# A gated attention and GLU kernel: key weights on one DMA queue, another order of the first key products, a shorter warm-up

## The chip, the cores and the metric

The kernel runs on one core of a Trainium2 chip. The metric is the device time of one execution in microseconds. The kernel before was run three times: 264.33, 264.85 and 264.85 us, median 264.85 us. The profile is of a further execution of 264.76 us, whose span (from the first to the last instruction that the profile shows) is 263.0 us, so 1.76 us of it lie around the span.

## The reference

`x` has 2048 tokens of 512 features, bfloat16. The output is a mixture per token of an attention with a memory (`a`) and a gated feed-forward layer (`b`):

```python
g = sigmoid((x * gate_w).sum(-1, keepdims=True))
out = g * a + (1 - g) * b
# a: 32 heads of 16, four segments of 512 tokens
q, k, v = x @ wq, x @ wk, x @ wv              # split into heads and segments
for s in range(4):
    a_dot = softmax(qs @ ks.T * scale + causal_mask) @ vs      # inside the segment
    a_mem = phi(qs) @ M / (phi(qs) @ z + 1e-6)                 # from earlier segments
    o = sigmoid(beta) * a_mem + (1 - sigmoid(beta)) * a_dot
    M, z = M + phi(ks).T @ vs, z + phi(ks).sum()
a = o @ wo
# b: 1792 hidden features
b = (gelu(x @ w_gate) * (x @ w_up)) @ w_down
```

## The kernel before

All the work is cut into named tasks, each a few instructions of one engine, and a string `ORDER` at the end of the file (L861) lists every task once. Each engine gets its tasks in that order and works them off strictly one after another; semaphores between the engines are derived from what each instruction reads and writes. A suffix in the string gives a choice: `xev0_0:d` puts the task on VectorE (`a` would be ScalarE), `K0_1a:1` takes PSUM bank 1. So the order is written out by hand, and nothing moves by itself. All loads start in SyncE's queue (SP) but two, which ScalarE's queue (ACT) starts.

The four segments go through the same stages: K, Q and V projections (`K`, `Q`, `V`), scores and exponentials (`st`, `exp`), products with V (`pv`), gate and up projections of the feed-forward part (`G`, `U`), down projection and output (`wo`, `out`, `oev`, `dma`). The string interleaves them, so that TensorE has dense products between the small ones of the attention.

The change lies in the head, the first 16 us, which only segment 0 has:

- The first half of the tokens of segment 0 is loaded straight, 128 tokens by SP (`ld_x0_0`) and 128 by ACT (`ld_x0_1`), L356 to L357. TensorE turns it: `xtr0_1`, the feature blocks 2 and 3, then `xtr0_0`, the blocks 0 and 1 (L785). The copies `xev0_1` and `xev0_0` carry the turned blocks from PSUM to `xT` (L793 on ScalarE, L794 on VectorE).
- The second half of these tokens comes by two transposing DMAs of SP, `ld_x0_t2` and `ld_x0_t3` (L361).
- The key weights `wk` come in two halves (L358): `ld_wk1` holds the feature blocks 2 and 3, `ld_wk0` the blocks 0 and 1.
- Behind them SP starts `ld_wq0`, `ld_wq1` (query weights, L364), `ld_gw` (`gate_w`, L363, which must wait until VectorE has zeroed `omem`, the task `gwz`, L354), `ld_beta` (L367, waits until wk0 has landed), `ld_wv` (L366, waits until `x0_t3` has landed), `ld_wg0` (the first half of the gate weights, 896 KB, L369, waits until wq1 has landed) and four transposing loads of the next segment's tokens (`ld_x1_*`, L345, wait until wq0 has landed).
- While nothing has landed TensorE multiplies constants, `warm1` before the turning and `warm2` behind it (L380 to L382).
- The keys of segment 0 (`K0_t`, L471 to L476) are made for four feature groups t in three parts each: `a` takes the blocks 2 and 3 (and so wk1 and `xev0_1`) for the first 256 tokens, `b` the blocks 0 and 1 (wk0 and `xev0_0`), `c` all four blocks for the other 256 tokens. That is 8 + 8 + 16 matmuls of 256 columns. `evict` (L441, L442) takes the sums out of PSUM.

Behind the keys TensorE does `Q0_0`, `Q0_1` (L448), the first scores `st0_0A` (L601), `gwtr`, `Q0_3`, then V products (L498), `st0_0B`, more V products, and then `G0_6` (L448), the first product that reads `wg`. TensorE's order does not let anything behind `G0_6` start ahead of it.

```python
    for eng, h in ((SP, 1), (ACT, 0)):
        ld_w(f"wk{h}", eng, wk[:, halves[h], :], wsrc(A_wk)[:, halves[h], :], [("wk", 2 * h), ("wk", 2 * h + 1)], 0.25)
```

Of the kernel before, what the change touches and what calls it, by code (L numbers as in the profile page):

```python
# [248 lines left out]
def _build(es, nc, A_x, A_wq, A_wk, A_wv, A_wo, A_beta, B_w_gate, B_w_up, B_w_down, gate_w, out):  # L249
# [30 lines left out]
    ident = sb("ident", [P, P])  # L280
# [77 lines left out]
    for eng, h in ((SP, 1), (ACT, 0)):  # L358
        ld_w(f"wk{h}", eng, wk[:, halves[h], :], wsrc(A_wk)[:, halves[h], :], [("wk", 2 * h), ("wk", 2 * h + 1)], 0.25)
# [21 lines left out]
    for name, n, cols in (("warm1", 45, 80), ("warm2", 7, 80)):  # L381
        one(name, PE, 3.0, [I(lambda e, cols=cols: e.matmul(BK[s0.i][:, 0:cols], ones, ones[:, 0:cols], start=True, stop=True),  # L382
                              [], [bk(s0)]) for _ in range(n)], bias=9000.0, opens=name == "warm1")
# [478 lines left out]
ld_x0_0 ld_wk1 ld_x0_1 warm1:0 ident xtr0_1 xev0_1:d xtr0_0 warm2 xev0_0:d vones0 masks ld_wk0 causal1 gwz ld_x0_t2  # L862
ld_x0_t3 ld_wq0 ld_wq1 ld_gw ld_beta causal0 consts K0_1a:1 K0_3a:2 K0_3b K0_2a:3 K0_0a:0 K0_2b K0_0b K0_1b K0_0c
K0_2c K0_3c K0_1c Kev0_0:d Kev0_2:d kpadb0_0 kpadb0_2 causal kpada0_0 Kev0_3:a Q0_0:0 Qev0_0:a Q0_1:3 st0_0A gwtr:2
Kev0_1:d gwev Q0_3:0 ld_wv ld_wg0 Qev0_1:d V0_1b:1 V0_3a:2 V0_3b:3 exp0_0A Qev0_3:d Vev0_3a:a Vev0_1b:a st0_0B
Vev0_3b:d kpada0_2 kpada0_1 V0_0b:0 V0_1a:2 V0_2a:1 Vev0_0b:d G0_6:3 Gev0_6:d Vev0_1a:d Vev0_2a:d exp0_0B st0_0C
exp0_0C Q0_2:0 G0_2:3 V0_2b:2 ld_x1_2 ld_x1_1 betab ld_x1_3 ld_x1_0 st0_0D Vev0_2b:a exp0_0D Gev0_2:d kpadb0_1
Qev0_2:d phka0_0 V1_2b:1 V0_0a:3 G1_6:2 V1_0b:0 Vev1_2b:d phka0_2 st0_0E Vev0_0a:d Vev1_0b:d G0_1:1 bexp Gev1_6:a
exp0_0E Gev0_1:d Q1_2:3 V1_3b:2 V1_3a:0 kpada0_3 Qev1_2:d Vev1_3a:d phkb0_2 phkc0_2 Vev1_3b:d st0_1A gz0 gqa exp0_1A
gr0 Q1_0:1 V1_0a:3 G1_5:0 Vev1_0a:d gqb Gev1_5:d st0_1B Q1_1:2 K1_0:3 exp0_1B phkb0_0 ld_wu1 ld_x2_0 G0_5:0 Qev1_0:d  # L870
kpadb0_3 vsh0_21 st0_1C exp0_1C Qev1_1:d ld_x2_1 ld_x2_3 ktr0_3 ld_wg1 Gev0_5:d V1_2a:1 K1_3:2 K1_1:0 vsh0_01
Vev1_2a:a vsh0_20 ld_x2_2 ktr0_2 vsh0_00 ld_wd1 st0_1D phkc0_0 Kev1_1:d kpada1_1 G0_4:1 G0_3:0 Gev0_4:d Kev1_0:d
Gev0_3:d Kev1_3:a ld_wd0 ld_wu0 ktr0_1 ktr0_0 vsh1_20 ld_wo V1_1a:2 Vev1_1a:d exp0_1D st0_2A exp0_2A msk0_0B msk0_0D
msk0_0C kpada1_0 msk0_0E goa0 gob0 msk0_0A msk0_1A msk0_1C msk0_1D gfull msk0_1B G0_0:1 Q1_3:3 G1_1:0 Qev1_3:d phqa1_0
st0_2B Gev0_0:d Gev1_1:a pv0_1:2301 exp0_2B tp0_d01 tp0_d00 pvp0_01 Q2_0:3 Qev2_0:d tp0_d11 st0_2C K1_2:2 Kev1_2:d
pvp0_00 tp0_d10 gelu0 G0_8:3 G0_13:1 gd0_13 G0_10:2 G0_11:0 G0_9:1 gd0_8 gd0_10 gd0_9 gd0_11 G0_12:3 G0_7:2 gd0_12
G1_2:1 U0_0:0 gd0_7 Gev1_2:d pvp0_11 h0_0 U0_13:3 U0_10:2 h0_10 Q2_1:1 Qev2_1:d exp0_2C st0_2D mz0:0 U0_7:2 U0_9:1
pvp0_10 h0_13 exp0_2D phqb1_0 st0_2E exp0_2E phka1_0 h0_7 mza0 h0_9 ota0_0 phqa1_2 kpadb1_0 G1_4:3 U0_1:2 h0_1
Gev1_4:a V1_1b:0 st0_3A G1_0:1 U0_5:3 Q2_2:2 exp0_3A Vev1_1b:a Gev1_0:a Qev2_2:a kpadb1_1 st0_3B exp0_3B U0_11:0
U0_4:1 U0_12:2 st0_3C phkb1_0 exp0_3C phqc1_0 kpada1_2 h0_4 h0_5 U0_6:1 U0_2:3 h0_11 h0_12 phqb1_2 h0_2 G1_3:0  # L880
Gev1_3:d h0_6 kpadb1_2 st0_3D phka1_2 U0_3:2 h0_3 U0_8:3 h0_8 Q2_3:0 Qev2_3:d exp0_3D phkb1_2 msk0_2A msk0_2B msk0_2C
msk0_3A msk0_2E msk0_2D msk0_3C goc0 msk0_3B st1_0A msk0_3D pv0_3:1230 exp1_0A st1_0B exp1_0B tp0_d20 tp0_d21 pvp0_20
tp0_d30 ota0_1 pvp0_21 tp0_d31 kpada1_3 out0_1_0:1 out0_1_1 out0_1_2 V2_0a:2 Vev2_0a:d G1_9:3 V2_1b:0 Vev2_1b:d
wev0_1:d st1_0C G1_8:2 G1_10:0 G1_11:1 gelu1 gd1_9 G1_7:3 gd1_8 gd1_10 gd1_7 gd1_11 G1_13:2 gd1_13 G1_12:0 gd1_12
phqc1_2 phkc1_0 mzq0 pvp0_31 pvp0_30 ota0_3 V2_0b:3 Vev2_0b:d ota0_2 V2_1a:1 Vev2_1a:d out0_0_0:2 out0_0_1 out0_0_2
nd1_0:0 ndp1_0 phkc1_2 exp1_0C st1_0D exp1_0D K2_0:3 K2_2:1 wev0_0:d Kev2_0:d Kev2_2:a K2_1:0 st1_0E Kev2_1:d U1_2:2
h1_2 wo0_1:1 nd1_3:3 nd1_1:0 exp1_0E st1_1A ld_x3_2 vsh1_00 vsh2_01 ktr1_1 ktr1_0 oev0_1 ndp1_1 wo0_0:2 oev0_0
kpada2_0 vsh1_21 out0_2_0:1 nd1_2:0 msk1_0C msk1_0A exp1_1A st1_1B exp1_1B msk1_0B gz1 msk1_0E msk1_1A msk1_0D msk1_1B
out0_2_1 wo0_2:2 ndp1_2 st1_1C exp1_1C nd1_5:0 out0_2_2 ndp1_3 wev0_2:a ndp1_5 out0_3_0:3 st1_1D nd1_4:0 out0_3_1
out0_3_2 ktr1_2 dma0 vsh1_01 otr1_3 ndp1_4 otr1_0 oev0_2 phka2_0 msk1_1C wev0_3:d ktr1_3 dma1 vsh2_00 otr1_1 ld_x3_1  # L890
ld_x3_0 ld_x3_3 exp1_1D st1_2A exp1_2A gr1 msk1_1D pv1_1:1023 st1_2B exp1_2B tp1_d01 tp1_d00 kpadb1_3 V2_2b:0
Vev2_2b:d K2_3:1 Kev2_3:a G2_3:0 pvp1_00 Gev2_3:d tp1_d10 st1_2C U1_8:1 G2_1:0 otr1_2 V2_3a:2 h1_8 Gev2_1:d Vev2_3a:d
kpadb2_0 kpadb2_1 exp1_2C st1_2D phkb2_0 exp1_2D G2_6:1 wo0_3:0 U1_3:2 pvp1_01 tp1_d11 Gev2_6:a h1_3 phka2_2 oev0_3
st1_2E U1_0:3 V2_3b:1 G2_0:2 Gev2_0:d h1_0 Vev2_3b:d exp1_2E phkb2_2 st1_3A mz1:0 G2_4:2 G2_5:3 pvp1_10 mza1 Gev2_5:d
exp1_3A st1_3B exp1_3B Gev2_4:d U1_11:1 G2_2:0 Gev2_2:d ota1_0 U1_13:3 h1_13 U1_10:2 h1_10 h1_11 G2_11:0 G2_10:3
pvp1_11 phkc2_0 phkc2_2 ota1_1 otm1_0 otm1_1 G2_12:2 G2_9:1 st1_3C gelu2 gd2_11 gd2_12 G2_7:0 G2_13:2 gd2_10 gd2_9
gd2_7 gd2_13 G2_8:3 gd2_8 U1_7:1 U2_9:0 K3_0:2 h1_7 U2_5:3 Q3_0:1 phqa2_0 h2_9 h2_5 Qev3_0:d Kev3_0:d exp1_3C st1_3D
exp1_3D U1_1:0 U2_12:3 msk1_3A msk1_2A msk1_3B U2_13:1 h2_12 h1_1 h2_13 kpada2_1 st2_0A U1_9:2 V2_2a:3 U2_7:0 msk1_2D
msk1_2B msk1_2E h1_9 Vev2_2a:d vsh2_20 dma2 dma3 ktr2_0 ktr2_2 vsh2_21 exp2_0A phqb2_0 msk1_3D msk1_2C msk1_3C st2_0B
h2_7 kpada2_2 pv1_3:1230 tp1_d21 exp2_0B tp1_d20 V3_1a:2 Vev3_1a:a st2_0C exp2_0C pvp1_21 tp1_d31 U1_6:1 Q3_1:2  # L900
V3_0a:0 st2_0D h1_6 pvp1_20 Vev3_0a:d Qev3_1:a V3_2b:1 U1_4:2 U1_5:0 exp2_0D st2_0E exp2_0E tp1_d30 phqc2_0 h1_5 h1_4
ota1_2 Vev3_2b:a U1_12:3 h1_12 pvp1_31 pvp1_30 out1_1_0:0 st2_1A V3_1b:2 out1_1_1 V3_3a:3 exp2_1A st2_1B msk2_0B
msk2_0D Vev3_3a:a exp2_1B out1_1_2 U2_4:1 msk2_0E goa1 gob1 kpadb2_3 kpada2_3 msk2_0C msk2_0A msk2_1A ota1_3 h2_4
otm1_2 otm1_3 K3_1:3 mzq1 Vev3_1b:a wev1_1:a st2_1C msk2_1B goc1 U2_1:2 Q3_3:1 V3_0b:0 Kev3_1:d kpada3_0 h2_1 Qev3_3:d
kpadb2_2 exp2_1C msk2_1C st2_1D V3_2a:3 U2_6:2 exp2_1D Vev3_2a:a wo1_1:1 Vev3_0b:d kpadb3_0 h2_6 oev1_1 st2_2A msk2_1D
pv2_1:0231 exp2_2A st2_2B exp2_2B tp2_d00 pvp2_00 phqa2_2 tp2_d01 tp2_d10 pvp2_10 pvp2_01 tp2_d11 out1_0_0:0 out1_0_1
st2_2C phqb2_2 out1_0_2 V3_3b:2 Vev3_3b:d wev1_0:d out1_3_0:3 phqc2_2 pvp2_11 exp2_2C st2_2D exp2_2D wo1_0:1 out1_3_1
st2_2E nd2_0:2 out1_2_0:0 out1_3_2 msk2_2C gz2 gr2 gz3 gr3 goa3 ndp2_0 gob3 oev1_0 msk2_2D goc3 goa2 gob2 exp2_2E
st2_3A exp2_3A msk2_3A msk2_2B wev1_3:d G3_4:2 nd2_2:1 out1_2_1 Gev3_4:a ndp2_2 st2_3B exp2_3B nd2_4:3 G3_1:1 Gev3_1:d
out1_2_2 nd2_1:2 st2_3C dma4 ktr2_1 vsh3_20 vsh3_01 ktr2_3 dma5 ndp2_4 ndp2_1 G3_3:1 wo1_3:3 exp2_3C Gev3_3:a K3_2:2  # L910
st2_3D wev1_2:a msk2_2A kpada3_1 oev1_3 Kev3_2:d nd2_5:1 nd2_3:3 G3_0:0 G3_5:2 ndp2_3 ndp2_5 Gev3_0:d msk2_3C msk2_2E
exp2_3D st3_0A exp3_0A goc2 msk2_3D msk2_3B G3_2:3 wo1_2:1 Gev3_2:d G3_6:0 Gev3_6:a Gev3_5:d oev1_2 ota2_0 st3_0B
pv2_3:3210 exp3_0B tp2_d20 tp2_d21 K3_3:3 Kev3_3:a pvp2_20 pvp2_21 U2_3:2 tp2_d30 h2_3 st3_0C U2_8:3 U2_0:1 tp2_d31
otr2_2 otr2_0 dma6 dma7 otr2_1 vsh3_00 otr2_3 vsh3_21 h2_0 ota2_1 G3_7:2 G3_12:0 G3_10:1 gelu3 gd3_7 h2_8 ota2_2
# [11 lines left out]
ndp3_4 ota3_1 dma11 otr3_2 otr3_1 otr3_3 otr3_0 pv3_3:1203 tp3_d20 tp3_d21 pvp3_20 pvp3_21 tp3_d30 tp3_d31 ota3_2  # L926
pvp3_31 pvp3_30 otm3_1 otm3_0 ota3_3 out3_0_0:1 out3_2_0:2 out3_0_1 out3_2_1 out3_3_0:0 out3_0_2 out3_3_1 wev3_0:a
otm3_2 otm3_3 wo3_0:3 dma10 oev3_0 dma12 wo3_1:1 out3_2_2 out3_3_2 wo3_2:3 oev3_1 wev3_2:a oev3_2 wo3_3b:1 dma13 dma14
wev3_3:a oev3_3b dma15b wo3_3a:2 oev3_3a dma15a
"""  # L930


# [26 lines left out]
```

## Time and profile before

| what | value |
|---|---|
| median of three runs (range) | 264.85 us (264.33 to 264.85) |
| profiled execution | 264.76 us |
| its span | 263.0 us |
| TensorE matmul busy | 255.4 us, 97% of the span |
| ScalarE, VectorE, GpSimd busy | 203.1, 197.7, 98.7 us |
| chain that ended last: TensorE, DMA, ScalarE, VectorE | 86%, 4%, 3%, 3% of the span |
| HBM read, written | 7.87 MB, 2.10 MB |
| first K0 matmul, first `G0_6` matmul | 5.20 us, 15.86 us from the start of the span |

Times on the page and in the views are in microseconds from the start of the span. A line of the timeline has the start, how long it lasted, the engine (SPq and ACTq are the queues that start DMAs), the line of the kernel, the operation, what it writes and reads, and in brackets the idle time of the engine ahead of it and what ended it. The chain of waits goes back from the last instruction to whatever released each step. A matmul's duration covers its way through the array, and matmuls overlap, so the distance from start to start tells their rate.

### The profile page before, as it was taken

The page shows a single profiled execution, that of the slowest core. Times are in us where ns is not written, and L with a number is a line of the kernel's source. Part 1 is how long each engine was busy: PE and PEld are TensorE (multiplying, and loading weights), DVE is VectorE, ACT ScalarE, POOL GpSimd, SP SyncE. Part 2 cuts the span into 40 slices and gives each one's busy share as a digit, 9 for nine tenths or more (in the row PEclk, how much of TensorE's full clock was granted, in tenths as well). Part 3 has the DMA queues.
Part 4 walks back from the last instruction along what each step waited for, and adds up shares of the span by engine and source line. Part 5 has one row for each costly group of instructions (what it writes and reads, how often), then busy time and mean ns, then how long its engine had stood idle before and what let it go on. Part 6 is the DMA issues. An engine that isn't in the chain of part 4 may idle for free.

```text
span 263.0 us, 6670 instructions
## 1 busy us (share of the span) xinstructions
PE 255.4 (97%) x2815; PEld 125.0 (48%) x2849; DVE 197.7 (75%) x412; ACT 203.1 (77%) x171; POOL 98.7 (38%) x163
## 2 busy tenths in 40 slices
PE   8999999999999999999999999999999999999995
PEld 8655445443464444544445445444544433544542
DVE  1668879285879686778968988976895973899873
ACT  1479879889998878898978898788788788677312
POOL 5006572024600465004706284156500477345300
PEclk9999999999999999999999999999999999999999
DMA  7794799200000212430003100022450000001412
GB/s 188 246 222 78 201 261 256 90 2 1 14 19 2 61 48 41 89 69 2 2 0 71 35 0 2 2 41 61 46 101 0 2 1 22 3 0 42 62 41 80
DMA packets 31974, 16.50 MB, mean 63 GB/s; under 512 B 21576, under 2 KB 31944, under 8 KB 31944
## 3 DMA queue, kind: packets, MB, share of 16 engines
q1 hardware_dynamic: 31528, 15.68, 26.8%
q8 instruction: 22, 0.36, 0.6%
q10 hardware_dynamic: 416, 0.39, 0.4%
q14 instruction: 8, 0.07, 0.1%
HBM read 7.87 MB, written 2.10 MB: 38 GB/s over the span
## 4 chain that ended last, share of the span: by engine, by line
PE 86%; DMA 4%; ACT 3%; DVE 3%; issue 2%; SPq 1%; DVEq 0%
PE psD L448 42%; PE psD L734 19%; PE psX L601 8%; PE psD L643 6%; PE psD L748 5%; PE psD L498 4%; DMA wg<-in_B_w_gate_dram 3%; PE psD L546 1%; ACT gb L697 1%; DMA wq<-in_A_wq_dram 1%; SPq L361 1%; ACT pt L608 1%; PE psD L576 1%; DVE vnat L505 1%; SPq L341 1%
## 5 line engine op out<-in xcount | busy, mean ns | idle before, releaser
L608 ACT ACTIVATE pt<-psX 128x2048 bf16<-128x2048 f32 x72 | 135.1, 1877 | 28.8 <-PE psX L601 27.3
L614 POOL TENSOR_TENSOR pt<-pt,ctri 128x256 bf16<-128x256 bf16 x128 | 92.2, 730 | 129.2 <-ACT pt L608 124.7
L448 PE MATMUL psD<-xT,wu 128*128 128x512 bf16 x214 | 52.7, 380 | 1.3 <-issue 1.1
L448 PE MATMUL psD<-xT,wg 128*128 128x512 bf16 x216 | 52.2, 379 | 1.0 <-issue 0.3
L734 PE MATMUL psD<-wd,gb 128*128 128x512 bf16 x217 | 51.8, 379 | 0.8 <-issue 0.5
L719 DVE TENSOR_TENSOR gb<-psD,gb 128x512 bf16<-128x512 f32 x56 | 37.2, 681 | 10.8 <-PE psD L448 10.8
L448 PEld LDWEIGHTS psD<-xT,wg 128*128 128x128 bf16 x224 | 20.7, 98 | 24.9 <-issue 1.3
L734 PEld LDWEIGHTS psD<-wd,gb 128*128 128x128 bf16 x224 | 20.7, 98 | 24.2 <-issue 2.1
L448 PEld LDWEIGHTS psD<-xT,wu 128*128 128x128 bf16 x224 | 20.2, 98 | 24.6 <-issue 2.6
L601 PE MATMUL psX<-qT,kD 32*128 32x192 bf16 (+7 forms) x512 | 28.5, 287 | 0.0
L529 DVE STREAM_TRANSPOSE tT<-psD 128x512 f32<-128x512 f32 x32 | 21.8, 702 | 5.8 <-PE psD L643 5.4
L442 DVE CAST gb<-psD 128x512 bf16<-128x512 f32 x20 | 13.6, 689 | 12.8 <-PE psD L448 12.7
L601 PEld LDWEIGHTS psX<-qT,kD 32*128 32x128 bf16 x512 | 8.2, 92 | 24.8 <-ACT pt L608 12.7
L498 PE MATMUL psD<-wv,xT 128*128 128x257 bf16 (+1 forms) x128 | 18.2, 273 | 0.0
L752 DVE SCALAR_TENSOR_TENSOR ost<-psD,gtok,wds 128x512 bf16<-128x512 f32 (+1 forms) x17 | 11.9, 712 | 7.9 <-PE psD L748 7.8
L643 PE MATMUL psD<-pt,vnat 64*17 64x128 bf16 (+7 forms) x512 | 17.7, 283 | 0.0
L702 ACT ACTIVATE gb<-psD 128x512 bf16<-128x512 f32 x28 | 15.0, 594 | 3.4 <-PE psD L448 3.3
L643 PE MATMUL psD<-pt,vsh 64*17 64x128 bf16 (+7 forms) x512 | 17.4, 283 | 0.0
L667 DVE SCALAR_TENSOR_TENSOR ob<-tT,gq,rc 128x256 bf16<-128x256 f32 x32 | 16.4, 513 | 1.1
L448 PE MATMUL psD<-xT,wq 128*128 128x512 bf16 x60 | 15.6, 379 | 0.3 <-issue 0.2
L748 PE MATMUL psD<-wo,oT 128*128 128x512 bf16 (+1 forms) x66 | 15.7, 367 | 0.2 <-issue 0.2
L498 PEld LDWEIGHTS psD<-wv,xT 128*128 128x128 bf16 x128 | 11.8, 97 | 6.5 <-issue 1.3
(81 smaller groups left out, 261.1 us busy)
## 6 DMA issues: line engine op xcount, KB each, us to landing
out_dram<-ost SPq DMA_DIRECT2D x15, 128.0 KB, 1.9
wg<-in_B_w_gate_dram SPq DMA_DIRECT2D x2, 896.0 KB, 6.4
wu<-in_B_w_up_dram SPq DMA_DIRECT2D x2, 896.0 KB, 8.1
wd<-in_B_w_down_dram SPq DMA_DIRECT2D x2, 896.0 KB, 7.7
vsh<-vnat SPq DMA_DIRECT2D x16, 68.0 KB, 2.4
wq<-in_A_wq_dram SPq DMA_DIRECT2D x2, 256.0 KB, 3.2
wv<-in_A_wv_dram SPq DMA_DIRECT2D x1, 512.0 KB, 5.0
wo<-in_A_wo_dram SPq DMA_DIRECT2D x1, 512.0 KB, 5.1
```

The lines of the kernel that those rows point to most:

```text
L448: one(name, PE, n * T_MM, [I(lambda e, i=i: e.matmul(BK[sl.i][:, :], lhs(i), rhs(i), start=(i == 0), stop=(i == n - 1)), reads(i), [bk(sl) ...
L498: one(f"V{s}_{m}{'ab'[hf]}", PE, 2 * T_MM, [I(lambda e, i=i, sl=sl, a=a, z=z, xs=xs: e.matmul(BK[sl.i][:, 0:z - a], xs(i), wv[:, i, a:z], ...
L529: one(f"tp{name}", DVE, 0.605, [I(lambda e, sl=sl, ti=ti: e.transpose(tT[ti][:, :], BK[sl.i][:, :]), [bk(sl)], [("tT", ti)])], bias=bias)
L601: ins.append(I(lambda e, t=t, kb=kb, ncol=ncol, c0=c0, g=g: e.matmul(XALL[:, g * 512 + c0:g * 512 + c0 + ncol], kD[(4 * s + t) % R_KD][32 ...
L608: one(f"exp{s}_{name}", ACT, 2048 * 0.000833 + 0.05, [I(lambda e: e.activation(pt[slot][:, :, :], xin, ACTF.Exp, scale=ATT_SCALE), [("X",) ...
L614: ins.append(I(lambda e, mv=mv: e.tensor_tensor(mv, mv, cm, ALU.mult), [("pt", slot), ("causal",)], [("pt", slot)]))
L643: ins.append(I(lambda e, kb=kb, slot=slot, c0=c0, n=n, g=g, r0=r0, sl=banks[j], va=va: e.matmul(BK[sl.i][32 * g:32 * g + 17, 64 * kb:512], ...
L667: I(lambda e, ti=ti, ri=ri, t=t, j=j, dst=dst: e.scalar_tensor_tensor(out=dst, in0=t_rows(ti), scalar=gq[:, 2 * t + j:2 * t + j + 1], in1= ...
L702: t = one(f"gd{s}_{ft}", ACT, 0.485, [I(lambda e, gi=gi, f=f, sl=sl: e.activation(gb[gi][:, f, :], BK[sl.i][:, :], ACTF.Gelu_apprx_tanh), ...
L719: one(f"h{s}_{ft}", DVE, 0.605, [I(lambda e, sl=sl, gi=gi, f=f: e.tensor_tensor(gb[gi][:, f, :], BK[sl.i][:, :], gb[gi][:, f, :], ALU.mult ...
L734: mm.append(I(lambda e, fb=fb, gi=gi, f=f, q=q, sl=sl: e.matmul(BK[sl.i][:, :], gb[gi][:, f, q], wd[:, fb, :], start=(fb == 0), stop=(fb = ...
L748: one(f"wo{s}_{qt}{sfx}", PE, 4 * T_MM * w / 512, [I(lambda e, kb=kb, q=q, so=so, c=c, w=w: e.matmul(BK[so.i][:, 0:w], oT[:, kb, q], wo[:, ...
```

## The change

Four edits, all in the head:

1. `ld_wk0` goes from ACT's queue to SP's, where it stands behind `ld_wk1` and ahead of `ld_x0_t2`.
2. `xev0_0`, the copy of the second turned half, goes from VectorE to ScalarE.
3. The parts `a` of all four K0 groups come ahead of all parts `b`.
4. `warm1` has 43 matmuls in place of 45, and the 7 of `warm2` have 48 columns in place of 80.

```diff
-    for eng, h in ((SP, 1), (ACT, 0)):
+    for eng, h in ((SP, 1), (SP, 0)):
         ld_w(f"wk{h}", eng, wk[:, halves[h], :], wsrc(A_wk)[:, halves[h], :], [("wk", 2 * h), ("wk", 2 * h + 1)], 0.25)
...
-    for name, n, cols in (("warm1", 45, 80), ("warm2", 7, 80)):
+    for name, n, cols in (("warm1", 43, 80), ("warm2", 7, 48)):
...
 ORDER = """
-ld_x0_0 ld_wk1 ld_x0_1 warm1:0 ident xtr0_1 xev0_1:d xtr0_0 warm2 xev0_0:d vones0 masks ld_wk0 causal1 gwz ld_x0_t2
-ld_x0_t3 ld_wq0 ld_wq1 ld_gw ld_beta causal0 consts K0_1a:1 K0_3a:2 K0_3b K0_2a:3 K0_0a:0 K0_2b K0_0b K0_1b K0_0c
+ld_x0_0 ld_wk1 ld_x0_1 warm1:0 ident xtr0_1 xev0_1:d xtr0_0 warm2 xev0_0:a vones0 masks ld_wk0 causal1 gwz ld_x0_t2
+ld_x0_t3 ld_wq0 ld_wq1 ld_gw ld_beta causal0 consts K0_1a:1 K0_3a:2 K0_2a:3 K0_0a:0 K0_1b K0_3b K0_2b K0_0b K0_0c
 K0_2c K0_3c K0_1c Kev0_0:d Kev0_2:d kpadb0_0 kpadb0_2 causal kpada0_0 Kev0_3:a Q0_0:0 Qev0_0:a Q0_1:3 st0_0A gwtr:2
...
```

The rest of the string is the same, word for word (the new file has it on one line).

## The prediction

> **What bounds the kernel now.** I read the shares of the chain on the page first, then the chain of waits in order of time for the first 30 us, where the change lies, then the timeline there. The shares come first:
>
> ```profile
> PE 86%; DMA 4%; ACT 3%; DVE 3%; issue 2%; SPq 1%; DVEq 0%
> ```
>
> TensorE carries the chain, but DMA and SP's queue hold 5%, and the chain of waits shows where (start, length, what):
>
> ```profile
> 1.25 0.41 SPq L341
> ...
> 1.71 1.28 SPq L361
> ...
> 3.04 1.26 SPq L361
> ...
> 4.34 0.58 SPq L341
> ...
> 4.97 3.17 DMA wq<-in_A_wq_dram
> ...
> 8.15 7.57 DMA wg<-in_B_w_gate_dram
> ...
> 15.86 0.38 PE psD L448
> ```
>
> The head is a chain of loads, not of products: SP starts wk1, the two transposing loads, wq0 and wq1; wq1 lands at 4.97 + 3.17 = 8.14; only then does SP start wg0, which lands at 8.15 + 7.57 = 15.72; then G0_6 runs. After 15.86 the chain has no DMA in it, so what G0_6 loses or gains the end loses or gains, unless a load is late there that was not before. The timeline tells how far TensorE itself is from this bound:
>
> ```profile
> 1.22 0.46 ACTq L341 DMA_DIRECT2D wk<-in_A_wk_dram  x1
> 4.44 0.85 DVE L794 COPY xT<-psX 128x512 bf16<-128x512 bf16 x2 [4.44 <-PE psX L785]
> 4.63 0.67 PE L382 MATMUL psD<-const-bfloat16-1.0 128*128 128x80 bf16 x7
> 5.20 4.38 PE L476 MATMUL psD<-xT,wk 128*128 128x256 bf16 x32
> 5.92 0.33 SPq L341 DMA_DIRECT2D omem<-in_gate_w_dram  x1
> 15.86 1.02 PE L448 MATMUL psD<-xT,wg 128*128 128x512 bf16 x3 [0.17 <-DMA wg<-in_B_w_gate_dram]
> ```
>
> The last V matmul ahead of G0_6 starts at 15.42 and takes 0.11 from start to start, so G0_6 could start at 15.53: TensorE waits 0.33 us for wg0 (0.17 of it with nothing in the array). SP's own waits, and the times from issue to landing (last number, us):
>
> ```profile
> SPq L341 <- DMA wq<-in_A_wq_dram: 1.0, 1, 1.0
> SPq L341 <- DVE omem L354: 0.5, 1, 0.5
> ```
>
> ```profile
> wk<-in_A_wk_dram ACTq DMA_DIRECT2D x1, 256.0 KB, 4.1
> wk<-in_A_wk_dram SPq DMA_DIRECT2D x1, 256.0 KB, 3.8
> pt<-in_A_x_dram ACTq DMA_DIRECT2D x1, 128.0 KB, 2.7
> ```
>
> **TensorE's start.** warm1 runs 45 matmuls from 0.82 to 3.78, 0.066 each; two fewer give 0.13. The tokens have landed by 0.79 + 2.7 = 3.49, so the turning can start at 3.65 instead of 3.78, and xev0_1 at 4.31; with half of the 0.85 for its copy it ends at 4.74. warm2 starts 0.13 earlier, at 4.50, and at 48/80 of 0.067 each its 7 matmuls take 0.28: done at 4.78. So K0 could start at about 4.83, not 5.20, if wk1 is there. Before, wk1 landed at 1.25 + 3.8 = 5.05, sharing the DMA engines with wk0 (landed 1.22 + 4.1 = 5.32); alone in front on one queue it should be there by 4.8, but that isn't shown. K0's start gains 0 to 0.37. Its first seven matmuls start about 0.21 apart up to 6.7, the later ones 0.11 apart, with the change of rate at 6.7 in either case; 0.37 us won in the slow part is worth half. TensorE gains 0 to 0.19; I take 0.15, as wk1's share of the traffic favours the upper end.
>
> **The second copy on ScalarE.** A 128x512 copy takes ScalarE 0.60 (the kT row) where VectorE takes 0.43. ScalarE's queue is free from its table load on, 1.28 us that start 0.46 sooner with wk0's issue gone. The copy would run from 4.73 to 5.33. With all `a` parts first, `b` starts only after eight matmuls of 0.21, at about 6.5: 1.2 us of cover for copy and wk0 both, so 0. If wk0 came later than 6.5, every 0.1 would cost 0.1 of TensorE's time, which is then still hidden as far as wg0 is late. VectorE is free 0.5 sooner, and `gwz`, which held SP by 0.5, no longer does.
>
> **SP's queue.** wk0's issue adds 0.41 and a gap of 0.05, so 0.46. All behind it move by that: t2 from 1.71 to 2.17, t3 from 3.04 to 3.50, wq0 from 4.34 to 4.80, wq1 from 4.97 to 5.43. At the gate weights the 0.5 wait soaks it up: SP is through with wq1 at 5.90 and starts them at 5.95 instead of 5.92, and beta and wv stay at 6.3 and 6.7. t3 (landing about 6.2 to 6.6) is not needed until part `c` at about 7.4. wq is not needed before Q0_0 at about 9.2, and 8.6 would do. But wg0's issue waits for wq1, and its data queue behind wq, beta and wv. This is the step that decides. Bounds: wq1 lands 0.46 later if its issue sets it, or 0 later if traffic sets it, because the same bytes go through the same engines. The DMA share by stretch speaks for something between (columns: us, busy time of each engine, clock, then DMA share and GB/s):
>
> ```profile
> 5.50:6.00 0.50, 0.50 (x4) 0.30 (x3) 0.22 (x2) 0.00 (x0) 0.00 (x0) 1.00 0.50 87
> 7.50:9.00 1.50, 1.50 (x17) 1.34 (x15) 0.70 (x2) 0.00 (x0) 0.00 (x0) 1.00 0.22 59
> 14.00:15.50 1.50, 1.50 (x20) 1.08 (x12) 1.39 (x6) 1.43 (x3) 0.00 (x0) 1.00 0.59 70
> ```
>
> The engines are full up to 5.5 (share 1.28 from 4.5 to 5.5) and then half empty until wq0 arrives: part of the 0.46 falls into time in which they were busy with the transposing loads anyway, part lengthens the hole. I take 0.30, nearer to the issue, as the hole shows that wq was not there. From 7.5 to 9.0 the engines run at 59 GB/s, while beta's small packets go ahead of wv; that stretch starts with the end of wq and so moves along. wg0 then ends with a slow tail (70 GB/s from 14.0 to 15.5): a few lanes finish late, and how late is not in my hands, ±0.3 or so by the 0.52 that the runs before differ.
>
> [...]
>
> **The sum.** wg0 lands at 15.72 + 0.30 = 16.02 and G0_6 starts at 16.16. TensorE would be ready at 15.53 - 0.15 = 15.38, so its 0.15 is not worth anything: its wait grows from 0.33 to 0.78. Nothing later absorbs the 0.30, as TensorE is 19.6 to 19.8 busy in every 20 us after that. The span becomes 263.3, the execution 264.76 + 0.30 = 265.06; the median of the runs stood 0.09 above the profiled one, so 265.15, say 265.1.
>
> **The rivals.** About 0.2%, 0.53 us, is what a measurement of this kernel can tell from no change.
> - The loads don't move: traffic sets wq1 and wg0 lands at 15.72 again. Then 264.85. For it: the full engines up to 5.5. Against: the hole after.
> - Faster: wg0 lands sooner because its tail is shorter when its data meet the others in another order. The most that this gives is TensorE's wait and its own gain, 0.33 + 0.19 = 0.52, so 264.3; the loads would have to land 0.5 sooner. Against: every load behind wk1 starts later or equal; for it: only the unsteady tail.
> - Slower by over 0.2%: all of the 0.46 passes, and the tail adds to it, for instance because wg0's data meet the x1 loads (started behind it) for longer. It decides once wg0 lands after 16.25. At 0.46 to 0.95 later, 265.3 to 265.8; I put the case at 265.6.
> - Slower by a cold clock: with less warming TensorE stands idle before K0 (up to 0.3, if wk1 lands at 5.05 again), and the fast rate does not come at 6.7. If the other 25 K0 matmuls all ran at 0.21, that is 25 x 0.10 = 2.5, less the 0.33 of cover: 267.0. Against: the hole would be short. [...]
>
> **How the numbers follow.** Forecast (wg0 0.1 to 0.5 later) 0.43; loads don't move 0.09; faster 0.18, of which 0.13 over 0.2% (a few of these need a gain that I don't see) and 0.05 within; slower by the tail 0.25; cold clock 0.05. So faster 0.13, same 0.43 + 0.09 + 0.05 = 0.57, slower 0.30. The forecast's own range is 264.9 to 265.4. The whole range reaches to 264.2 on the faster side and 265.8 on the slower, and leaves out the cold clock and some of either end.
>
> **What would show it.** K0's first matmul at 4.8 to 4.9 (TensorE's start right), wk1 landed by 4.8; SP's t2 issue at 2.17 and wq1's at 5.43; gate weights at about 5.95 without a wait for VectorE; wq1 landed at 8.3 to 8.6; wg0 at 15.9 to 16.2; a wait of about 0.8 ahead of G0_6. I am wrong if wg0 lands by 15.7 or sooner, if G0_6 no longer waits for a DMA, or if K0 runs at 0.21 past 7 us.

## The result and the profile after

| | median of 15 runs (range) | profiled execution | its span |
|---|---|---|---|
| before | 264.53 us (263.99 to 264.85) | 264.76 us | 263.0 us |
| after | 265.68 us (264.88 to 266.65) | 265.20 us | 263.5 us |

The changed kernel takes 1.0045 times as long, 95% interval 1.0033 to 1.0057: 1.15 us more by the medians, slower by more than a measurement of this kernel can tell from no change. The profiled execution of after is near the low end of its runs, so its trace shows only part of the loss.

The shares of the chain on the page of the changed kernel, by engine:

```profile
PE 84%; DVE 4%; DMA 4%; ACT 3%; issue 2%; SPq 2%; DVEq 0%
```

They hardly differ. The chain of waits of the changed kernel, from SP's second load to G0_6 (start, length, what):

```profile
1.25 0.41 SPq L341
...
1.71 0.46 SPq L341
...
2.21 1.29 SPq L361
...
3.55 1.26 SPq L361
...
4.85 0.58 SPq L341
...
5.47 3.46 DMA wq<-in_A_wq_dram
...
8.94 6.76 DMA wg<-in_B_w_gate_dram
...
15.75 0.39 PE psD L448
```

The second line is the new one, wk0's issue. What stands behind it on SP, up to wq1, is 0.50 us later (the gate weights, which had waited for VectorE before, only 0.06), and wq1 lands at 5.47 + 3.46 = 8.93, 0.79 later than before. But wg0 takes 6.76 where it took 7.57, so in this execution G0_6 starts at 15.75, 0.11 sooner than before. The timeline of the changed kernel's head:

```profile
4.46 0.42 DVE L794 COPY xT<-psX 128x512 bf16<-128x512 bf16 x1 [4.46 <-PE psX L785]
4.89 0.60 ACT L793 ACTIVATE xT<-psX 128x512 bf16<-128x512 bf16 x1 [2.38 <-PE psX L785]
4.96 4.19 PE L476 MATMUL psD<-xT,wk 128*128 128x256 bf16 x32
5.98 0.41 SPq L341 DMA_DIRECT2D omem<-in_gate_w_dram  x1
15.75 1.04 PE L448 MATMUL psD<-xT,wg 128*128 128x512 bf16 x3 [0.48 <-DMA wg<-in_B_w_gate_dram]
```

K0 starts at 4.96 (before 5.20) and G0_6 waits 0.48 us for wg with nothing in the array (before 0.17). SP's own wait for data in the changed kernel, its loads from issue to landing, and the stretches shown before:

```profile
SPq L341 <- DMA wq<-in_A_wq_dram: 1.6, 1, 1.6
```

```profile
wk<-in_A_wk_dram SPq DMA_DIRECT2D x2, 256.0 KB, 3.6
wq<-in_A_wq_dram SPq DMA_DIRECT2D x2, 256.0 KB, 3.4
pt<-in_A_x_dram ACTq DMA_DIRECT2D x1, 128.0 KB, 3.0
```

```profile
5.50:6.00 0.50, 0.50 (x5) 0.30 (x4) 0.00 (x0) 0.00 (x0) 0.00 (x0) 1.00 1.42 249
7.50:9.00 1.50, 1.50 (x16) 1.34 (x15) 1.12 (x2) 0.25 (x1) 0.00 (x0) 1.00 0.57 178
14.00:15.50 1.50, 1.27 (x12) 0.87 (x9) 0.96 (x5) 1.50 (x1) 0.00 (x0) 1.00 0.66 135
```

The wait for VectorE ahead of the gate weights is gone. The stretch from 5.5 to 6.0, in which wk0 now lands (5.73), is full (share 1.42, before 0.50), and the thin stretch of beta's small packets starts later. In the last line TensorE is busy for 1.27 of 1.50: it has run out of products and waits for wg0.

So the head ends early by 0.11, and the execution still ends late. Both traces put side by side further on keep this lead for 165 us: the first product behind the scores at 180 us starts at 180.30 in after, 180.40 in before. Then it is lost. The chain of waits of the kernel before, from 186 us, has one unbroken run of V products (L643, the task `pv2_3`):

```profile
188.75 2.14 PE psD L643 x121
...
191.04 1.67 PE psD L448 x7
```

In the changed kernel the chain leaves these products after 64 of them and goes by VectorE, while TensorE itself works on to 190.6 and stops; the next L448 product starts at 191.47. The chain names VectorE here because its reciprocal (L666, 191.13 to 191.34) is the last thing to end ahead of that product, but the product does not need it: in the kernel before the same reciprocal starts at 191.22, behind the product at 191.04.

```profile
188.65 1.21 PE psD L643 x64
...
189.89 1.31 DVE tT L529 x2
...
191.47 1.67 PE psD L448 x7
```

The timeline of TensorE's weight loads and products in the changed kernel shows what happened there:

```profile
190.57 0.19 PE L643 MATMUL psD<-pt,vnat 64*17 64x64 bf16 x1
191.11 0.09 PEld L643 LDWEIGHTS psD<-pt,vnat 64*17 64x17 bf16 x3 [0.51 <-issue]
191.12 0.20 PE L643 MATMUL psD<-pt,vnat 64*17 64x64 bf16 x3 [0.35 <-issue]
```

In the middle of a group of four equal products TensorE stops after the first and takes the other three half a microsecond later. No semaphore, buffer or load is named ("issue" is time in which the engine waited for nothing that the profile shows). Another record differs there, that of the DMA queue q8, called instruction: 22 packets in 263 us (0.36 MB, so 16 KB each), which by the name bring instructions; that they are TensorE's is inferred from a count further down. (A second queue of that name, q14, moves too, near here at 188.09 in before and at 184.46 in after, but not with the stop.) The queue in the stretch from 185.5 to 187.5 us, kernel before (packets, MB, share):

```profile
q8 instruction: 1, 0.02, 4.7%
```

In the changed kernel this stretch has none, and the packet comes between 187.5 and 190:

```profile
q8 instruction: 1, 0.02, 2.7%
```

Its start is at 186.93 in before and at 188.84 in after. That became the third theory below.

### The profile page after: what moved, and what is told of

The parts are those of the page before. It is cut to its first block, busy times and chain, and to the rows that moved or that the text cites. A ratio compares the mean times of both kernels' runs of the same rounds, so it can differ in the third digit from the quotient of the medians.

```text
span 263.5 us, 6666 instructions
## 1 busy us (share of the span) xinstructions
PE 255.1 (97%) x2813; PEld 124.5 (47%) x2847; DVE 196.9 (75%) x411; ACT 203.8 (77%) x172; POOL 99.2 (38%) x163
## 4 chain that ended last, share of the span: by engine, by line
PE 84%; DVE 4%; DMA 4%; ACT 3%; issue 2%; SPq 2%; DVEq 0%
PE psD L448 41%; PE psD L734 19%; PE psX L601 8%; PE psD L643 6%; PE psD L748 5%; PE psD L498 4%; DMA wg<-in_B_w_gate_dram 3%; PE psD L546 1%; DMA wq<-in_A_wq_dram 1%; ACT gb L697 1%; DVE tT L529 1%; SPq L361 1%; ACT pt L608 1%; PE psD L576 1%; SPq L341 1%
## 5 line engine op out<-in xcount | busy, mean ns | idle before, releaser
L448 PE MATMUL psD<-xT,wu 128*128 128x512 bf16 x214 | 52.7, 380 | 1.3 <-issue 1.1
L448 PE MATMUL psD<-xT,wg 128*128 128x512 bf16 x216 | 52.3, 379 | 1.3 <-DMA wg<-in_B_w_gate_dram 0.5
L448 PEld LDWEIGHTS psD<-xT,wg 128*128 128x128 bf16 x224 | 20.7, 98 | 25.3 <-issue 1.3
L448 PEld LDWEIGHTS psD<-xT,wu 128*128 128x128 bf16 x224 | 20.2, 98 | 24.7 <-issue 2.6
L601 PE MATMUL psX<-qT,kD 32*128 32x192 bf16 (+7 forms) x512 | 28.5, 287 | 0.0
L601 PEld LDWEIGHTS psX<-qT,kD 32*128 32x128 bf16 x512 | 8.2, 92 | 24.8 <-ACT pt L608 12.7
L643 PE MATMUL psD<-pt,vnat 64*17 64x128 bf16 (+7 forms) x512 | 17.8, 283 | 0.4 <-issue 0.4
L643 PE MATMUL psD<-pt,vsh 64*17 64x128 bf16 (+7 forms) x512 | 17.3, 283 | 0.0
L448 PE MATMUL psD<-xT,wq 128*128 128x512 bf16 x60 | 15.6, 379 | 0.4 <-issue 0.2
```

Source lines behind the costliest of these rows:

```text
L448: one(name, PE, n * T_MM, [I(lambda e, i=i: e.matmul(BK[sl.i][:, :], lhs(i), rhs(i), start=(i == 0), stop=(i == n - 1)), reads(i), [bk(sl) ...
L601: ins.append(I(lambda e, t=t, kb=kb, ncol=ncol, c0=c0, g=g: e.matmul(XALL[:, g * 512 + c0:g * 512 + c0 + ncol], kD[(4 * s + t) % R_KD][32 ...
L643: ins.append(I(lambda e, kb=kb, slot=slot, c0=c0, n=n, g=g, r0=r0, sl=banks[j], va=va: e.matmul(BK[sl.i][32 * g:32 * g + 17, 64 * kb:512], ...
```

## The experiments

The ratios are to the kernel before, run beside each on the same chip. The theories that the expectations speak of:
- **A, the queue:** wk0's place on SP moves wq1 and wg0, and all of the loss is G0_6's wait.
- **B, the warming:** the shorter warming costs TensorE's clock.
- **C, the instructions:** four fewer TensorE instructions (two matmuls, each with its weight load) move the borders of the blocks in which, by this theory, TensorE's instructions come (the 16-KB packets of q8); one block comes late and TensorE stands still near 191 us. The first four expectations have it in a plainer form, taken from the trace of the changed kernel (TensorE runs dry once because its stream is shorter); blocks and borders came in behind those four.

**Edit 1 undone in the changed kernel.**

```diff
-    for eng, h in ((SP, 1), (SP, 0)):
+    for eng, h in ((SP, 1), (ACT, 0)):
```

> The changed kernel with the one load wk0 back on ScalarE's queue; the other three edits stay. Theory A (SP's queue: wk0's issue moves wq1 and so wg0 back, the gate weights then land later than 15.7 us in most executions): back to the time before or a little under, 264.3 to 264.6 us, wq1 landed at about 8.1 us in the profile. Theory B (shorter warming costs TensorE the fast clock early): the loss stays, 265.3 to 265.8 us. Theory C (TensorE runs dry of instructions once, near 191 us as in the changed kernel's profile, 0.5 us, because its instruction stream is four instructions shorter): the loss stays at about 0.5, 265.0 us.

Measured: 267.93 us (267.31 to 269.08), ratio 1.0139, interval 1.0113 to 1.0164. The experiment missed its aim. In the changed string `ld_wk0` stands behind `xev0_0:a`, so that on ACT the issue waits until the copy of the second turned half has started (4.74). The timeline of this run:

```profile
4.75 0.39 ACTq L341 DMA_DIRECT2D wk<-in_A_wk_dram  x1
8.46 4.45 PE L476 MATMUL psD<-xT,wk 128*128 128x256 bf16 x24 [2.08 <-DMA wk<-in_A_wk_dram]
```

wk0 leaves at 4.75 where it left at 1.22 before, and 24 of the 32 K0 products wait for it until 8.46. The stretches of the same run show a second price (after the busy times: granted clock, DMA share, GB/s):

```profile
6.00:8.00 2.00, 0.37 (x4) 0.09 (x1) 0.00 (x0) 0.00 (x0) 0.00 (x0) 1.00 1.01 336
9.50:12.50 3.00, 3.00 (x16) 2.11 (x14) 1.92 (x6) 0.38 (x1) 0.00 (x0) 0.50 0.69 227
```

The clock is 1.00 while TensorE is idle and 0.50 from 9.31 to 12.73, in the middle of its work (the means of the stretches beside it, 0.81 from 9.0 to 9.5 and 0.92 from 12.5 to 14.0, give the same two ends). What follows: edits 1 and 2 belong together, since ScalarE can't take the copy and issue wk0 early in this order. The run does not tell A from B. C asks for a stop near 191 us here too, and there is none; this exception is taken up below the table.

**Edit 1 alone in the kernel before.**

```diff
-    for eng, h in ((SP, 1), (ACT, 0)):
+    for eng, h in ((SP, 1), (SP, 0)):
```

> The kernel before with the one load wk0 moved to SP's queue, nothing else changed. Theory A: the whole loss, 265.4 to 265.8 us; wq1 lands at 8.6 to 8.9 us. Theory B: no change, 264.4 to 264.6 us. Theory C: no change in TensorE's stream, so no loss, 264.4 to 264.6 us.

Measured: 264.94 us (264.19 to 265.49), ratio 1.0007, interval 0.9993 to 1.0020. The head does what A says (timeline of this run):

```profile
16.05 1.02 PE L448 MATMUL psD<-xT,wg 128*128 128x512 bf16 x4 [0.88 <-DMA wg<-in_B_w_gate_dram]
```

wq1 lands at 8.60, wg0 at 15.91, G0_6 starts at 16.05, 0.19 later than before, and the span is 0.2 longer. That is the prediction's step, a little smaller; but it is not the loss that was measured. As the whole cause, A falls.

**Edit 4 alone in the kernel before.**

```diff
-    for name, n, cols in (("warm1", 45, 80), ("warm2", 7, 80)):
+    for name, n, cols in (("warm1", 43, 80), ("warm2", 7, 48)):
```

> The kernel before with the shorter warming alone (43 matmuls of 80 columns and 7 of 48). Theory A: no change, 264.3 to 264.6 us, because the gate weights still land at 15.7 us. Theory B: 265.2 to 265.8 us. Theory C: TensorE's stream is the changed kernel's, so about 0.5 us more, 265.0 us, with a wait for nothing visible of 0.5 us behind 188 us in the profile.

Measured: 265.57 us (264.73 to 266.28), ratio 1.0039, interval 1.0027 to 1.0052. The warming alone gives nearly the whole loss. Its timeline has the same stop, longer (0.97; K0 gained nothing, it waited for wk1 until 5.25):

```profile
191.88 0.09 PEld L643 LDWEIGHTS psD<-pt,vnat 64*17 64x17 bf16 x3 [0.97 <-issue]
```

By time alone B could still have been the reason; but a cold clock would cost in the head (with edit 1 undone it lay at 9.31 to 12.73), and this stop is 186 us behind the warming.

**The changed kernel again, unaltered.**

> The changed kernel unaltered, beside the others on the same chip, for a second profile: 265.7 us. Theory A: wq1 lands at 8.6 to 9.0 us again and wg0 anywhere from 15.6 to 17 us, and the span follows wg0's landing. Theory C: a wait of TensorE of 0.5 us near 191 us is there again, whenever wg0 lands.

Measured: 266.07 us (265.74 to 266.33), ratio 1.0058, interval 1.0041 to 1.0074. wq1 lands at 8.60, wg0 at 15.96, G0_6 starts at 16.01, and the stop near 191 us is 0.94. So the 15.75 and the 0.51 of the first trace are the good end of both.

**The count restored in the changed kernel, the length of the warming not** (45 matmuls of 76 columns are 3420 columns, 43 of 80 are 3440).

```diff
-    for name, n, cols in (("warm1", 43, 80), ("warm2", 7, 48)):
+    for name, n, cols in (("warm1", 45, 76), ("warm2", 7, 48)):
```

> The changed kernel with 45 first warming matmuls of 76 columns in place of 43 of 80: the warming lasts the same (3420 columns against 3440), TensorE has as many instructions as in the kernel before. Theory C (the stream of TensorE's instructions is fetched in blocks, and with four fewer the block that holds the products with V near 191 us is fetched 2 us later and comes too late): the wait near 191 us is gone, the fetch falls at 187 us again, 264.5 to 264.9 us. Theory B (less warming time): no difference from the changed kernel, 265.7 to 266.1 us. Theory A (SP's queue): 265.7 to 266.1 us.

Measured: 265.15 us (264.32 to 265.82), ratio 1.0031, interval 1.0016 to 1.0046. The stop near 191 us is gone, and the instruction packet starts at 188.02, with G0_6 0.33 later than before. The kernel is still slower than before, now by its head (timeline of this run):

```profile
16.19 1.04 PE L448 MATMUL psD<-xT,wg 128*128 128x512 bf16 x3 [1.47 <-DMA wg<-in_B_w_gate_dram]
```

**The count lowered in the kernel before, the length of the warming kept** (3612 columns for 3600; in the chain of waits the first warming takes 3.17 us here and 3.16 with 45 of 80 in the run after this one). This is C alone: nothing but the number of instructions changes.

```diff
-    for name, n, cols in (("warm1", 45, 80), ("warm2", 7, 80)):
+    for name, n, cols in (("warm1", 43, 84), ("warm2", 7, 80)):
```

> The kernel before with 43 first warming matmuls of 84 columns in place of 45 of 80: four instructions fewer, the warming as long as before (3612 columns against 3600). Theory C: the whole loss of the shorter warming, 265.4 to 265.7 us, with a wait of 0.5 to 1.0 us near 191 us. Theory B: no change, 264.5 us.

Measured: 265.42 us (264.89 to 266.14), ratio 1.0047, interval 1.0029 to 1.0065. The timeline of this run:

```profile
190.80 0.09 PEld L643 LDWEIGHTS psD<-pt,vnat 64*17 64x17 bf16 x3 [0.98 <-issue]
```

The instruction packet starts at 188.04, and between 185.5 and 187.5 there is none. With the loads, the copy, the order of K0 and the length of the warming all as before, four instructions fewer bring a stop of 0.98 us at 191 us. The medians differ by as much (265.42 to 264.44); the ratio's interval is 0.8 to 1.7 us. So it is shown that the number of instructions alone brings the stop and the loss. That a late block is the means is inferred from the packets, which are put side by side below the table.

**The count of before with the narrower second warming.** This is B without C.

```diff
-    for name, n, cols in (("warm1", 45, 80), ("warm2", 7, 80)):
+    for name, n, cols in (("warm1", 45, 80), ("warm2", 7, 48)):
```

> The kernel before with the second warming at 48 columns in place of 80, the number of matmuls unchanged: 0.19 us less warming and no instruction fewer. Theory C: no change, 264.4 to 264.7 us, no wait near 191 us. Theory B: part or all of the loss, 265.0 to 265.6 us.

Measured: 264.72 us (264.18 to 265.22), ratio 1.0017, interval 1.0006 to 1.0028. No stop, and the packet is early (186.22). The profiled execution was itself a short one (span 262.5), so what the 0.17% is stays open. This run takes 0.19 of the 0.32 us that edit 4 takes from the warming; in the kernel before, the first warming was not shortened with its count kept. As the main cause B falls.

**Beta's load on ACT's queue, with the count restored.** Beta goes in 64-byte pieces and wv stands behind it on SP.

```diff
-    ld_w("beta", SP, ball, A_beta.partition_broadcast(P), [("ball",)], 0.02, ["wk0"])
+    ld_w("beta", ACT, ball, A_beta.partition_broadcast(P), [("ball",)], 0.02, ["wk0"])
```

> The changed kernel with 45 first warming matmuls of 76 columns, and with the load of beta, whose 128 packets of 64 bytes stand ahead of wv on SP's queue, moved to ScalarE's queue. If the time of the head is set by wg0's landing and beta holds up the loads behind it: wv lands at about 10 us, wg0 before 15 us, G0_6 starts at 15.1 to 15.4 us instead of 15.75 to 16.05, and the time is 263.8 to 264.2 us. If beta's packets cost the same on either queue: 264.5 to 264.9 us.

Measured: 264.56 us (264.01 to 265.41), ratio 1.0009, interval 0.9997 to 1.0021. wv landed at 11.42, not near 10 as expected, so beta's place in the queue isn't what holds wv. wg0 landed at 15.41 and G0_6 started at 15.46; the time is that of before within its interval, not below it.

**G0_6 later, in the kernel before and in the changed kernel with the count restored.** G0_6 and Q0_2 change places, with their copies and banks: the first product that needs wg comes 1.3 us later.

```diff
-Vev0_3b:d kpada0_2 kpada0_1 V0_0b:0 V0_1a:2 V0_2a:1 Vev0_0b:d G0_6:3 Gev0_6:d ...
+Vev0_3b:d kpada0_2 kpada0_1 V0_0b:0 V0_1a:2 V0_2a:1 Vev0_0b:d Q0_2:3 Qev0_2:d ...
-exp0_0C Q0_2:0 G0_2:3 ...
+exp0_0C G0_6:0 G0_2:3 ...
-Qev0_2:d phka0_0 ...
+Gev0_6:d phka0_0 ...
```

> The kernel before with G0_6, the first product that reads the gate weights, and Q0_2 in each other's place (each with its eviction and the other's PSUM bank), so that G0_6 comes about 1.3 us later and TensorE should not wait for wg0. TensorE has as many instructions as before. If the span follows G0_6's wait: 0.3 to 0.5 us less, 264.0 to 264.2 us, and no wait for the gate weights in the profile. If something else would be late next (the next segment's tokens at 16 to 19 us): no change, 264.5 us.

> The changed kernel with 45 first warming matmuls of 76 columns, and G0_6 and Q0_2 in each other's place. If its loss without the wait near 191 us (265.15 us measured) is the wait for wg0, 1.6 us in that profile, of which a late wg0 makes up to 0.8: 263.8 to 264.2 us, below both kernels. If it is not: 265.0 us or more.

Measured: in the kernel before 264.27 us (263.66 to 265.28), ratio 0.9992, interval 0.9975 to 1.0010; in the changed one with 45 matmuls 264.24 us (263.64 to 265.44), ratio 0.9989, interval 0.9970 to 1.0008. The timeline of the latter:

```profile
16.22 1.90 PE L448 MATMUL psD<-xT,wg 128*128 128x512 bf16 x8
19.36 1.05 PE L498 MATMUL psD<-wv,xT 128*128 128x257 bf16 x8 [0.48 <-DMA xT<-in_A_x_dram]
```

G0_6 starts at 16.22 without a wait for wg; the next load that is late is that of the second segment's tokens. Against the same kernel without the exchange (1.0031) the loss is gone, so that loss was the wait for wg0. This version is 1.4 us quicker than the changed kernel by medians taken at different times, but it isn't shown to be quicker than before.

**Two other counts, in the kernel before** (one time each, so no interval).

```diff
-    for name, n, cols in (("warm1", 45, 80), ("warm2", 7, 80)):
+    for name, n, cols in (("warm1", 44, 82), ("warm2", 7, 80)):
```

> The kernel before with 44 first warming matmuls of 82 columns in place of 45 of 80 (two instructions fewer, warming as long). One look at where the block of instructions is fetched: with the theory of the blocks it is fetched at 168 and 187 us as before, or at 170.5 and 189 us as with 43, according to where the block's border falls; a wait near 191 us goes with the second alone.

```diff
-    for name, n, cols in (("warm1", 45, 80), ("warm2", 7, 80)):
+    for name, n, cols in (("warm1", 47, 77), ("warm2", 7, 80)):
```

> The kernel before with 47 first warming matmuls of 77 columns in place of 45 of 80 (four instructions more, warming as long). With the theory of the blocks the border falls earlier in the work, so the fetches are at 168 and 187 us or sooner and there is no wait near 191 us; if any other number of instructions than the one before brings the wait, it is there too.

Measured: 264.88 us with 44 and 264.30 us with 47. Both lie within the range of the kernel before (263.65 to 266.52), so only the traces count here. With 44 the timeline has the stop:

```profile
190.78 0.09 PEld L643 LDWEIGHTS psD<-pt,vnat 64*17 64x17 bf16 x4 [1.05 <-issue]
```

With 47 there is none, and the packet starts at 186.38. Four loads wait here where three waited with 43: one matmul and one load more ahead of it moved the stop one matmul and one load earlier in the program, as it would with blocks of a fixed number of instructions.

**One marker for all.** From the traces, the span is G0_6's start plus 247.2 us plus the stop near 191 us, to within 0.1, with the order of before at G0_6:

| kernel | warm1 matmuls | G0_6 starts | stop near 191 us | sum | span |
|---|---|---|---|---|---|
| before | 45 | 15.86 | 0 | 263.1 | 263.0 |
| after | 43 | 15.75 | 0.51 | 263.5 | 263.5 |
| edit 1 undone | 43 | 18.85 | 0 | 266.1 | 266.0 |
| edit 1 alone | 45 | 16.05 | 0 | 263.3 | 263.2 |
| edit 4 alone | 43 | 16.05 | 0.97 | 264.2 | 264.2 |
| after again | 43 | 16.01 | 0.94 | 264.2 | 264.2 |
| after, count restored | 45 | 16.19 | 0 | 263.4 | 263.4 |
| before, 43 wider | 43 | 14.97 | 0.98 | 263.2 | 263.2 |
| before, narrower warm2 | 45 | 15.28 | 0 | 262.5 | 262.5 |
| beta on ACT | 45 | 15.46 | 0 | 262.7 | 262.7 |
| before, 44 wider | 44 | 14.89 | 1.05 | 263.1 | 263.2 |
| before, 47 narrower | 47 | 15.19 | 0 | 262.6 | 262.6 |

Two terms make every span: when G0_6 starts, and whether TensorE stops near 191 us. The first varies by itself (14.89 to 16.05 in the six rows with all loads as before, 15.75 to 16.19 in the four that differ from them by edit 1 with wk0 early). In four of those six (14.89 to 15.28) G0_6 does not wait for wg0 at all; TensorE itself comes to it then. The second is a matter of count, with one exception. The run with edit 1 undone has 43 matmuls and no stop. Its packet starts 171.8 us after G0_6 where the other kernels with 43 or 44 have 172.9 to 173.4 and those with 45 or 47 170.9 to 171.8.

What sorts all 14 traces, this run too, is the packet against the V products of `pv2_3`. In the five with a stop it starts 0.02 to 0.54 us behind the first of their weight loads, in the nine without one 1.0 to 2.0 us ahead of it. From the packet's start to the first instruction behind the stop it is 2.3 us (after), 2.5 (44), 2.7 (after again), 2.8 (43 wider) and 3.0 (edit 4 alone). From its end it is 1.2 to 1.5 us, while in the nine others the same instruction comes 1.8 us or more after it. So in all five the packet has ended some 0.4 to 0.7 us before TensorE stops (in after it ends at 189.92, and the last load ahead of the stop at 190.60), and what still passes between its end and the next instruction no trace shows. Why the packet of the run with edit 1 undone starts earlier than those of the same count is open.

## Why the prediction was right or wrong

- **The range and the sign.** 265.68 lies inside 264.2 to 265.8, near its upper end; the case held likeliest, within 0.2%, was not the outcome, and 265.1 was 0.6 too low. It came out slower, as in the rival by wg0's tail, and near the 265.6 that it was given, but not by that rival: wg0 landed at 15.70, 15.91, 15.96 and 16.14 in the four profiles with edit 1 and wk0 early, not after 16.25. The stop near 191 us is in no term of the sum and in no rival; that the time fell inside the range all the same is in that part luck.
- **The step that failed: the warming.** "two fewer give 0.13" booked the removed matmuls as time won and priced the smaller number of instructions at nothing. The runs put 0.5 to 1.0 us in its place: ratio 1.0047 (1.0029 to 1.0065) for the count alone. The step "Nothing later absorbs the 0.30" looked for cover behind the head, and rightly found none; it did not ask whether something later could be hurt. No row of the trace of before shows the stop, but the 22 packets of the instruction queue were on its page.
- **Why it is that block.** 5664 weight loads and matmuls in 22 packets of 16 KB, in the kernel before, are 257 per packet, if the packets are TensorE's and full; that is the author's estimate, and how many blocks TensorE holds at a time no run shows. The V products of `pv2_3` are 128 matmuls with 128 loads, 256 together and so about a whole block, and run through in about 2.1 us (2.14 in the chain of before), less than the 2.3 to 3.0 us that pass from the packet's start to the first instruction of the next block in the traces with a stop. By these numbers the packet of the next block has to start before they begin: that was at 186.93 in before, 1.75 ahead of their first load (188.68), and at 188.84 in after, 0.26 behind it (188.58).
- **TensorE's start.** Forecast 4.83, measured 4.96. The tokens landed at 0.79 + 3.0 = 3.79 instead of 3.49, with the turning behind them; wk1 was there by 4.40, in time as forecast. K0's end moved by 0.42 instead of 0.15, because the rate rose at 6.1 instead of 6.7. That it would rise at 6.7 in either case was the author's assumption, and no run shows a fixed time. As said, none of it counted: G0_6 waited for wg0.
- **The second copy.** 4.89 to 5.49 on ScalarE, forecast 4.73 to 5.33; wk0 landed at 5.73, with `b` at 6.37. Hidden, 0, right. What it ties to edit 1 (the issue of wk0 behind the copy) I had not said; the first experiment paid 3.4 us for it.
- **SP's queue.** The shift was 0.50 instead of 0.46 (t2 2.21, wq1 5.47, gate weights 5.98 without a wait). wq1 landed at 8.93, 8.60, 8.60 and 8.52 in the four profiles (after, after again, edit 1 alone, count restored), forecast 8.3 to 8.6, so 0.38 to 0.79 later: nearer to all of the issue's time than to a part of it. Against the one profile of before, wg0 was then 0.0 to 0.4 later, forecast 0.30. But that profile was a late one of its kind. That the head is "a chain of loads, not of products" holds for it, but not for the four rows of the table with the loads of before in which G0_6 does not wait for wg0. G0_6 starts at 15.37 in the mean of the six rows with the loads of before and at 16.00 in the mean of the four with edit 1, 0.63 later. So the term was of the right kind and may be up to twice the 0.30; edit 1 alone, at 1.0007 (0.9993 to 1.0020, at most 0.53 us), speaks for the smaller size, the changed kernel with its count restored (1.0031) for the larger. That the wait for wg0 is what costs there is shown by the pair with and without the exchange of G0_6.
- **Cold clock.** It did not happen in the changed kernel: the rate rose sooner, not later. No run shows a cause for that: K0's slow start (0.21 from product to product) lasts from none to seven products in the profiles, with no order by the warming (none with edit 4 alone, five and six in the two of the changed kernel, seven before). In the run with edit 1 undone it did, from an idle TensorE: 2.08 us without a product ahead of 8.46, and then 3.42 us at half the clock (0.50 from 9.31 to 12.73). With edit 4 alone TensorE stood idle for 0.59 us ahead of K0, and its first seven products started 0.11 apart (from 5.25 on). Which length between the two is enough was not shown.
- **What stays open.** The loss with the count restored (1.0031) and the loss by the count alone (1.0047) add up to 0.78%, more than the 0.45% and 0.58% measured for both together; they fit only near the lower ends of their intervals (0.16 + 0.29). So how the loss divides between count and queue is known to some tenths of a us and no better. Why four instructions move the packet by 2 us is not shown. By the estimate of 257 a packet the border ahead of the one with the stop lies three or four pairs of load and matmul ahead of the first V product with 43 and five or six with 45, so among the eight scores (L601, 188.25 in after) both times, and what sets the packet's start can't be read from that. Moving a wait there by itself was not tried. Edits 2 and 3 were not run alone. The 0.17% of the narrower second warming has no cause yet.

## What to carry to other kernels

Here four instructions fewer of 5664 on the engine that bounds the kernel cost 0.47% (0.29 to 0.65). So in a long straight stream take the number of instructions as part of the layout: where it can be kept, keep it (here warming can be shortened by columns), and after any edit look for "issue" waits inside a run of equal products and at where the instruction packets start. The stop fell into a run of tiny instructions, 256 in 2.1 us. Compare two traces by one marker just behind the edit and one far behind it, so that a loss 186 us away is not put down to the place of the edit; and where a load goes to another queue, count what stands ahead of it there.

## What the runs showed of the hardware

- In five traces (after, after again, edit 4 alone, 43 wider, 44 wider) TensorE stood still for 0.51 to 1.05 us near 191 us, with three products of a group of four still to come, with 44 all four. It went on 2.3 to 3.0 us after a 16-KB packet of the instruction queue q8 had started, and 1.2 to 1.5 us after that packet had ended (it took 1.0 to 1.5 us). The profile calls the wait "issue".
- With edit 1 undone, an idle stretch of 2.08 us in the head was followed by half the clock (0.50) from 0.85 us after the work had resumed (8.46), for 3.42 us (9.31 to 12.73).
- Beta's load of 8 KB in 64-byte pieces took 3.8 to 3.9 us to land; from 7.5 to 9.0 us of it the DMA engines moved 59 GB/s in the kernel before. Taking it out of SP's queue left wv at 11.42 all the same.
- With all loads as in the kernel before, wg0 took from 6.1 to 7.7 us from issue to landing in different profiles, more than any part of the edit moved it. A single pair of traces can't size a step that ends on such a load.
